# Reordering the opening of a fused forward-and-backward kernel: which load, which product and which table come first

## The chip, the cores and the metric

The kernel runs on one core of one Trainium2 chip. The metric is the device time of one execution in microseconds (us), lower is better. The core has a matrix engine (TensorE; PE in the profile, its weight loads PEld), a vector engine (VectorE, DVE), a scalar engine (ScalarE, ACT), a general engine (GpSimd, POOL) and a queue engine that issues most transfers (SyncE, SP). Each engine works through its own instructions in a fixed order and waits on semaphores for the others. PSUM is the memory that TensorE writes to; a result there is "evicted" by VectorE or ScalarE. Chip memory is reached by DMA only.

## What is computed

The reference is a block with a spectral mixer and an MLP, both modulated by a condition vector `c`, together with all its gradients (one sequence of 2048 rows, width 512, MLP width 1792, bfloat16):

```python
mod = (silu(c) @ w_mod).reshape(1, 6, 1, -1)
sa, ca, ga, sb, cb, gb = (mod[:, i] for i in range(6))
h = layernorm(x) * (1 + ca) + sa
x = x + ga * irfft2(rfft2(h) * (w_r + 1j * w_i))
h = layernorm(x) * (1 + cb) + sb
x = x + gb * (relu(h @ w1 + b1) ** 2 @ w2 + b2)
# outputs: x and, for grad_out, the gradients of A_x, w_r, w_i, w1, b1, w2, b2, c, w_mod
```

## The kernel before

**Stages.** The 2048 rows are 16 tiles of 128 rows, handled in pairs, and four blocks `b` of four tiles. The Fourier transforms are products with sine tables that the kernel makes itself: GpSimd writes integer patterns (`iota`), VectorE turns them into phases (a multiply-add and a bitwise and), ScalarE takes `Sin`. The tables are `TA`/`TAT` (`build_ta`), `Cd` (`build_cd`), the middle table `LF` (`build_lf`, four quarters `q`, patterns from `iotas_lf`) and `Cf` (`build_cf`).

**The opening** is this. `c` and `b1` are loaded into one small tile `vrow` (L560, L561), turned to columns by one TensorE transpose into `vrow_ps` (L589), and ScalarE makes the sigmoid (L590) and `scb`, silu(c) repeated over 128 columns (L593). `mod_row(j)` (L604) is one of the six modulation rows: four products of 512 columns with a 512-column part of `w_mod` (tile `wm`), spread over all partitions and evicted into `modb`. Row 1 is `ca`, row 5 is `gb`. `gb` is then needed as a column over partitions, so four one-column products turn row 5 round (L621) and VectorE doubles it into `gb2x` (L623).

**The row stage** works on pairs of row tiles: statistics (`row_stats`, L638 and L639 on VectorE, then four small GpSimd operations), normalisation (`row_norm`, L650 on VectorE or L652 on ScalarE), times 1+ca (L656), a fold (`fold1`, L250 and L251), and the first transform (`spec_f1_half`, L286 and L287, into `psA`), evicted by ScalarE into `UT` (L288, `utcs`).

**The fill.** The gradient of the MLP's inner layer, `grad_out` times `w2` transposed, needs nothing of the forward path. Both operands come by transposing DMAs: `w2T` (L580, two halves) and `gT[b]` (L577, one per block, in two buffers, so that block 2 waits for the products of block 0 and block 3 for those of block 1). VectorE scales `gT[b]` by `gb2x` (`scale_g`, L629). `back_products(b)` then makes 14 results `fc` of four products each (L714), 56 a block and 224 in all, evicted into `gab`: every third by VectorE (L717), the others by ScalarE (L719). They have a very late priority, so the scheduler puts them into gaps of TensorE that it expects.

**What follows.** Modulation rows 0, 4, 3, 2 and a row `dcrow` made of them (L692, L693); `spec_f23`, the two further transforms for eight groups `gi` (L324, evicted to `AE` by L329; L310, evicted to `Xs` by L312), each followed by a complex product with the spectral weights (`cmul`, L420 to L423); `spec_g1` (L345, L358), `spec_g2` (L376, `Tsb` L379) and `spec_g3` (L387) back; the second layernorm; then the MLP forward (L886), back, and the weight gradients, to the end. The first L886 product stands behind all 224 fill products.

**What sets the order.** A scheduler orders the instructions of each engine when the program is built, from its own estimates and from priorities: `tc.high_priority()` pulls a part forward, `Priority(tc, LATE)` pushes it back, and `with tc.issue_after(K[...])` keeps an instruction behind a named one. Transfers on SP and ScalarE are issued in the order of that engine's instructions, so a wait of one holds back those behind it. Tiles of a pool share `bufs` buffers: a new tile waits until the last reader of the one that it replaces is done.

## Time and profile before

| | |
|---|---|
| time, three runs | 419.98, 422.49, 424.95 us (median 422.49) |
| span of the profiled execution (first to last instruction) | 416.3 us; a time of its own is not listed beside the span |
| TensorE clock granted | 1.000 |
| busy share: PE, PEld, DVE, ACT, POOL | 94, 47, 83, 67, 15% |
| data moved by DMA | 101.11 MB, 243 GB/s on average |
| share of the largest DMA queue (q1) | 84.1% of 16 engines |
| `gT` (block 0) transposing DMA, time on SP's queue | 6.85 us from 2.22 |
| first product of the row stage; first fill product | 14.60; 16.27 us |

A line of the profile's groups or of its instructions in order of time has: the start, the time of one or several instructions, engine, source line, operation, tile written, tiles read, shape, count, and in brackets how long the engine had stood idle before and what ended that. An "xN" joins N instructions; their times overlap by the pipeline of the engine, so the distance of two starts is often shorter than the time of one.

### The profile page before, as it was taken

To read this page: it belongs to the slowest core of one execution; us is meant where nothing else is said; L and a number is where in the kernel's file an instruction comes from. 1 tells how busy PE (TensorE), PEld (TensorE's weight loads), DVE (VectorE), ACT (ScalarE), POOL (GpSimd) and SP (SyncE) were. 2 spreads that over 40 slices of the span, in tenths; PEclk is the share of its full clock that TensorE was granted. 3 is DMA by queue.
4 is the path that set the end of the run, shared out by engine and by line. 5 is a ranking of instruction groups with operands and counts; after the bars stand their busy time and mean duration, and the time that the engine had idled before them with its cause. 6 is when DMAs were issued, how large, how long until landed. Compare 5 with 4: busy or idle time off the path is not lost. (4 is left out here: it accounts for less than half of the span.)

```text
span 416.3 us, 7175 instructions
## 1 busy us (share of the span) xinstructions
PE 391.7 (94%) x2387; PEld 197.6 (47%) x2407; DVE 343.7 (83%) x827; ACT 277.1 (67%) x495; POOL 60.6 (15%) x147
## 2 busy tenths in 40 slices
PE   2789999999899999999999999999999999999996
PEld 0345445664444444444444444445555665444444
DVE  6899868977988578988897998964999784877885
ACT  4568699868884079338924776545655567897785
POOL 7437950000000000000000000001314520000000
PEclk9999999999999999999999999999999999999999
DMA  8999899979199459949976997998999999999994
GB/s 240 232 261 298 237 213 313 323 239 240 40 331 324 126 161 276 248 128 204 288 227 194 201 291 278 291 213 245 287 280 283 350 265 227 223 269 223 239 266 143
DMA packets 143923, 101.11 MB, mean 243 GB/s; under 512 B 99049, under 2 KB 126830, under 8 KB 143630
## 3 DMA queue, kind: packets, MB, share of 16 engines
q1 hardware_dynamic: 140394, 92.96, 84.1%
q0 software_dynamic: 2784, 7.10, 5.6%
q10 hardware_dynamic: 708, 0.59, 0.5%
q8 instruction: 19, 0.31, 0.3%
q14 instruction: 18, 0.15, 0.1%
HBM read 35.44 MB, written 41.60 MB: 185 GB/s over the span
## 5 line engine op out<-in xcount | busy, mean ns | idle before, releaser
L714 PE MATMUL mm<-gT,w2T 128*128 128x512 bf16 x224 | 57.9, 382 | 4.5 <-ACT gab L719 4.2
L1144 PE MATMUL mm<-gab,h_sb 128*128 128x448 bf16 x256 | 50.9, 352 | 0.0
L1232 PE MATMUL mm<-g_sb,hn 128*128 128x512 bf16 (+1 forms) x250 | 49.6, 352 | 0.8 <-ACT gw L1234 0.4
L915 PE MATMUL og<-w1T,gab 128*128 128x512 bf16 x219 | 49.9, 379 | 0.3
L915 PE MATMUL og<-w,h 128*128 128x512 bf16 x216 | 49.1, 379 | 0.4
L886 PE MATMUL mm<-h2T,w 128*128 128x512 bf16 x164 | 40.2, 379 | 0.5 <-ACT r L888 0.3
L1232 PEld LDWEIGHTS <-hn 128*128 128x128 bf16 x256 | 24.4, 98 | 23.4 <-issue 2.0
L1144 PEld LDWEIGHTS <-h_sb 128*128 128x128 bf16 x256 | 24.6, 98 | 21.8 <-issue 0.8
L886 PEld LDWEIGHTS <-w 128*128 128x128 bf16 x224 | 21.3, 98 | 27.7 <-issue 4.9
L915 PEld LDWEIGHTS <-h 128*128 128x128 bf16 x224 | 21.7, 98 | 25.6 <-DVE h L890 0.6
L915 PEld LDWEIGHTS <-gab 128*128 128x128 bf16 x224 | 21.6, 98 | 25.5 <-DVE gab L894 1.0
L714 PEld LDWEIGHTS <-w2T 128*128 128x128 bf16 x224 | 21.2, 98 | 24.2 <-issue 7.9
L888 ACT ACTIVATE r<-mm,b1col 128x512 bf16<-128x512 f32 x41 | 27.4, 688 | 6.3 <-DVE gab L894 3.3
L294 POOL MEMSET AE<- 128x2 bf16 x4 | 0.3, 103 | 188.5 <-DMA gh_dram<-gab 188.5
L928 ACT CAST G<-og 128x512 bf16<-128x512 f32 x16 | 9.2, 580 | 22.2 <-PE og L915 22.2
L329 ACT ACTIVATE AE<-psB 128x1024 bf16<-128x1024 f32 x16 | 21.8, 1363 | 1.8 <-PE psB L324 0.9
L719 ACT CAST gab<-mm 128x512 bf16<-128x512 f32 x36 | 21.0, 593 | 2.6 <-PE mm L714 2.3
L890 DVE TENSOR_TENSOR h<-r 128x1024 bf16<-128x1024 bf16 x28 | 19.2, 686 | 2.6 <-ACT r L888 2.5
L1148 ACT CAST gw<-mm 128x448 bf16<-128x448 f32 x16 | 8.6, 537 | 18.4 <-PE mm L1144 18.4
L477 DVE SCALAR_TENSOR_TENSOR gm_junk<-wmc,onef,gmbc 128x512 bf16<-128x512 bf16 x24 | 18.0, 750 | 3.3 <-ACT gmbc L467 2.2
L894 DVE TENSOR_TENSOR gab<-r,gab 128x1024 bf16<-128x1024 bf16 x28 | 19.2, 684 | 0.0
L379 ACT ACTIVATE Tsb<-psT 128x512 bf16<-128x512 f32 x32 | 18.5, 603 | 0.6 <-ACT utcs L368 0.5
(292 smaller groups left out, 818.5 us busy)
## 6 DMA issues: line engine op xcount, KB each, us to landing
h_dram<-h SPq DMA_DIRECT2D x28, 256.0 KB, 3.2
gh_dram<-gab SPq DMA_DIRECT2D x28, 256.0 KB, 3.6
w<-in_B_w_dram SPq DMA_DIRECT2D x2, 1792.0 KB, 9.0
wmc<-in_w_mod_dram SPq DMA_DIRECT2D x12, 256.0 KB, 5.8
wz_dram<-Z SPq DMA_DIRECT2D x8, 258.0 KB, 3.8
xs_dram<-Xs SPq DMA_DIRECT2D x8, 258.0 KB, 4.0
Z<-wz_dram SPq DMA_DIRECT2D x8, 258.0 KB, 6.0
Xb<-xs_dram SPq DMA_DIRECT2D x8, 258.0 KB, 8.2
```

The source lines that it names most:

```text
L329: nc.scalar.activation(dst, ps.rearrange("p r (s e f) -> p (r s) e f", s=2, e=2), AF.Copy, scale=EF_S)
L379: K["Tsb"] = nc.scalar.activation(Tsb, ps, AF.Copy, scale=EF_S).ins
L477: nc.vector.scalar_tensor_tensor(out=junk, in0=wmc[:, i, :], scalar=K["onef"], in1=gmbc, op0=ALU.mult, op1=ALU.mult, accum_out=self.gsc[:, ...
L714: nc.tensor.matmul(ps, lhsT=w2T[:, dc, fc * P:(fc + 1) * P], rhs=gT[b][:, :, dc, :], start=(dc == 0), stop=(dc == 3))
L719: nc.scalar.copy(out=gaT[b][:, fc, :], in_=ps)
L886: nc.tensor.matmul(ps, lhsT=w1[:, dc, (fc + i) * P:(fc + i + 1) * P], rhs=h2T[b][:, :, dc, :], start=(dc == 0), stop=(dc == 3))
L888: nc.scalar.activation(r[:, i, :], ps, AF.Relu, bias=b1col[:, fc + i:fc + i + 1])
L890: nc.vector.tensor_tensor(h2, r, r, op=ALU.mult)
L894: K["gh"] = nc.vector.tensor_tensor(gh, r, gh, op=ALU.mult).ins
L915: nc.tensor.matmul(ps, lhsT=lhs(fc), rhs=rhs[:, fc, :], start=(fc == 0), stop=(fc == NFC - 1))
L1144: nc.tensor.matmul(ps[:, 0:W4], lhsT=h2_sb[:, t, dc * P:(dc + 1) * P], rhs=ghn[t // 4][:, t % 4, fs], start=(t == 0), stop=(t == NT - 1))
L1232: nc.tensor.matmul(ps[:, 0:w], lhsT=hns[fc][:, t, :], rhs=g_sb[:, t, c:c + w], start=(t == 0), stop=(t == NT - 1))
```

## The change

- Loads: `c` goes first on SP's queue, alone; `b1` goes into a tile of its own (`brow`) on ScalarE's queue. Then the first four row tiles, the weights of row 5, `gT[0]`, the weights of row 1, and `w2T` in three pieces (3, 4 and 7 of its 14 parts) with the later row tiles between and behind them.
- The gate column: instead of row 5, its eviction and four one-column products, sixteen one-column products of the weights with the column `sc` = silu(c). Row 5 is made later, after the row stage. The transpose of `b1` goes there too.
- `scale_g(0)` no longer stands behind the statistics; `scale_g(2)` stands behind a product of the row stage in place of the phases of `LF`.
- `build_lf` is split: `build_lf_phase` (phases and `Sin`, now straight into `LF`) is written ahead of the row stage; the multiplication by signs and masks stays where it was, in place. The patterns for it are made first on GpSimd.
- Four small PSUM tiles share one name, `sm_ps`, with two buffers. `TA` is held behind the sigmoid.

```diff
@@ build_ta
+    with tc.issue_after(K["sig"]):
+        nc.scalar.activation(TA[:, 0], v, AF.Sin, scale=TWO_PI / 128, bias=K["npi"])
...
+def build_lf_phase(tc, K, cpool, g, krs):
...
+    for q in range(4):
+        v = g.tile([P, 2, 4, P], I16, name="lf_v", bufs=2)
+        for i in range(2):
+            V.tensor_scalar(v[:, i], krs[q].rearrange("p a h x u -> p (a h) (x u)"), t, ph[:, i:i + 1], op0=ALU.mult, op1=ALU.add)
+        if q == 0:
+            V.tensor_scalar(v[:, :, 0, 2:64:4], v[:, :, 0, 2:64:4], 512.0, None, op0=ALU.add)
+        K["lf_v"] = V.tensor_single_scalar(v, v, 2047, op=ALU.bitwise_and).ins
+        K["lf_w"] = nc.scalar.activation(LF[:, 4 * q:4 * q + 4, 0:2, :], v.rearrange("p i n x -> p n i x"), AF.Sin,
+                                         scale=TWO_PI / 2048, bias=K["npi"]).ins
...
@@ the opening
-    nc.scalar.dma_start(vrow[0:4, :], c.rearrange("b (dc p) -> (b dc) p", p=P))
-    nc.scalar.dma_start(vrow[4:4 + NFC, :], B_b1.rearrange("(fc p) -> fc p", p=P))
+    nc.sync.dma_start(vrow, c.rearrange("b (dc p) -> (b dc) p", p=P))
...
-    nc.sync.dma_start(x_sb[:, 0:4, :], x_view[:, 0:4, :])
-    nc.sync.dma_start(wmt[0][:, :, D:2 * D], wm_view[:, :, D:2 * D])
-    nc.scalar.dma_start(wmt[2][:, :, D:2 * D], wm_view[:, :, 5 * D:6 * D])
-    nc.sync.dma_start(x_sb[:, 4:8, :], x_view[:, 4:8, :])
...
+    load_x(0, 4)
+    load_mod(5)
+    load_gT(0)
+    load_mod(1)
+    load_w2T(0, 3)
+    load_w2T(3, 7)
+    load_x(4, 4)
+    load_w2T(7, NFC)
+    load_x(8, 4)
+    load_x(12, 4)
+    nc.scalar.dma_start(brow, B_b1.rearrange("(fc p) -> fc p", p=P))
+    load_mod(4)
+    load_gT(1)
+    load_mod(0)
+    load_wm(1)
+    load_gT(2)
+    load_gT(3)
...
+        K["sig"] = nc.scalar.activation(sigcol, pv, AF.Sigmoid).ins
+        nc.vector.tensor_copy(ccolf, pv)
+        sc = p0.tile([P, 4], BF16, name="sc")
+        nc.vector.tensor_tensor(sc, sigcol, ccolf, op=ALU.mult)
...
+    build_ta(tc, K, constp, gen, psM)
+    build_cd(tc, K, lfp, gen)
+    lf_io, lf_kr = iotas_lf(tc, gen)
+    cf_dr = iota_cf(tc, gen)
+    lf_ph = build_lf_phase(tc, K, lfp, gen, lf_kr)
...
-        mod_row(1)
-        mod_row(5)
-        psc = psM.tile([P, 4], FP32, name="modc_ps", bufs=1)
+        psc = psM.tile([P, 4], FP32, name="sm_ps")
         for cc in range(4):
-            nc.tensor.matmul(psc[:, cc:cc + 1], lhsT=modb[0:1, GB_B, cc * P:(cc + 1) * P], rhs=K["ones_col"][0:1, :], start=True, stop=True)
+            for dc in range(4):
+                nc.tensor.matmul(psc[:, cc:cc + 1], lhsT=wmt[2][:, dc, D + cc * P:D + (cc + 1) * P], rhs=sc[:, dc:dc + 1], start=(dc == 0), stop=(dc == 3))
         gb2x = constp.tile([P, 4], FP32, name="gb2x")
         nc.vector.tensor_scalar(gb2x, psc, 2.0, None, op0=ALU.mult)
+        mod_row(1)
...
-            with tc.issue_after(K[("stats", "stats", "lf_v", "cmul")[b]]):
+            with tc.issue_after(K[("stats", "stats", "f1v", "cmul")[b]]) if b else ExitStack():
...
     row_stats(0)
+    scale_g(0)
...
-        for j in (0, 4, 3, 2):
+        for j in (0, 4, 3, 2, 5):
             mod_row(j)
+        pb = psM.tile([P, NFC], BF16, name="sm_ps")
+        nc.tensor.transpose(pb, brow, K["ident"][0:NFC, 0:NFC])
+    nc.vector.tensor_copy(b1col, pb)
...
-    build_lf(tc, K, lfp, gen, *lf_io)
+    build_lf(tc, K, gen, lf_io, *lf_ph)
```

In the program as it is built after the change, the orders that matter are these. TensorE: transposes, the sixteen products, row 1, 34 fill products, then the first transform; 66 fills stand ahead of the last transform (66 before the change too), 89 ahead of the dc row's use (84 before), 116 at the end of `spec_f23` (144 before), 126 at the end of `spec_g1` (150 before). VectorE: three phases ahead of `TA`'s copies, the rest between the first statistics and the first fill evictions, three fill evictions ahead of the first fold; the scaling of `gT[3]` inside the last `cmul`. ScalarE: row 1's eviction, three `Sin`, two fill evictions, the fourth `Sin`. SP: the DMA of `gT[3]` behind the sixth `xs_dram` store, where it waits for the last product of block 1, fill 112.

## The prediction, made before the changed kernel was run

> **What bounds the kernel now.** I read the page first, then busy time by stage, the instructions in order of time on each engine, and what TensorE waited for.

> ```profile
> PE 391.7 (94%) x2387; PEld 197.6 (47%) x2407; DVE 343.7 (83%) x827; ACT 277.1 (67%) x495; POOL 60.6 (15%) x147
> ```

> TensorE is busy for 94% of the span, so a microsecond is won or lost only where TensorE stands idle. I cut the span at its own milestones: first row transform (14.60), last one (41.20), dc row (50.70), inverse transform (79.87), its row step (89.70), first forward MLP product (113.77).

> ```profile
> core 0: us, PE busy (x) PEld busy (x) DVE busy (x) ACT busy (x) POOL busy (x), PEclk, DMA share, GB/s
> 0.00:14.60 14.60, 4.44 (x15) 1.36 (x15) 9.75 (x54) 6.75 (x12) 9.87 (x54) 1.00 0.99 245
> 14.60:41.20 26.60, 23.74 (x130) 13.20 (x131) 24.56 (x68) 19.32 (x34) 14.38 (x32) 1.00 1.02 264
> 41.20:50.70 9.50, 9.45 (x65) 4.25 (x63) 8.06 (x41) 6.78 (x12) 9.03 (x16) 1.00 0.83 239
> 50.70:79.87 29.17, 27.04 (x193) 15.85 (x192) 22.93 (x64) 27.70 (x42) 6.68 (x12) 1.00 1.04 267
> 79.87:89.70 9.83, 9.82 (x103) 7.19 (x104) 9.26 (x18) 5.51 (x10) 0.00 (x0) 1.00 1.01 346
> 89.70:113.77 24.07, 22.47 (x139) 10.95 (x140) 19.23 (x48) 20.69 (x41) 0.00 (x0) 1.00 0.57 140
> ```

> The second stage is VectorE's (24.56 of 26.60), the fourth ScalarE's (27.70 of 29.17). The 224 products of L714 (the "fill": gradient times w2T) are spread between these stages by the scheduler, and all of them stand ahead of the first forward product, before and after. Busy TensorE is flattered by pipelining, so I count work by spacing: twelve fill products take 2.75 us, (2.75-0.38)/11 = 0.215 us each; a 256-column product 0.11, a 128-column one 0.055. By that, the second stage holds 66 fills and 64 transforms, 14.2+7.0 = 21.2 us in 26.6: 5.4 us are idle. The stage from 50.70 holds 23.8 in 29.2; the last 21.0 in 24.1.

> The opening is a chain of waits:

> ```profile
> 5.81 0.17 PE L589 MATMUL vrow_ps<-ident,vrow 18*128 18x18 bf16 x1 [5.81 <-DMA vrow<-in_B_b_dram]
> 10.88 1.87 PE L604 MATMUL mod_ps<-wm,scb 128*128 128x512 bf16 x4 [0.78 <-ACT modb L606]
> 13.75 0.26 PE L621 MATMUL modc_ps<-ones_col,modb 1*128 1x1 bf16 x4 [1.00 <-ACT modb L610]
> 14.60 0.39 PE L286 MATMUL psA<-TA,fold_u 128*128 128x256 bf16 x1 [0.59 <-DVE fold_u L250]
> 23.79 2.75 PE L714 MATMUL mm<-gT,w2T 128*128 128x512 bf16 x12 [0.36 <-ACT gab L719]
> ```

> **The change, step by step.** *Opening.* c goes first, without b1, so the transpose need not wait for the second small load; from c's issue at 0.75 the sigmoid can start up to some 1.3 us sooner, but this ends no wait that I price, since the gate column then waits for its weights. SP's queue gains three issues (c, the gate weights, one more w2T piece) of about 0.41 us (row L567), which delay the first x by 0.45. The gate column replaces mod_row(5), its eviction and four products by sixteen one-column products. Bytes ahead of the gate weights shrink to c and one x tile: 1.05 MB. 142 GB/s in the first five us and 333 in the next five put that at 6.0; the first x tile, 3.7 by the same count, was waited for until 5.41 (1.7 more), so I take 7.4. Sixteen one-column products have no row; below, four L621 took 0.26 us (0.065 each, so 1.0); above, mod_row's weight loads follow at 0.25 to 0.32 (so 4 to 5). I take 0.1, nearest to the 98 ns of a weight load: 1.6. The gate scale is then ready at about 9.0 instead of 14.05.

> [...]

> *VectorE.* The four table phases are moved from 40 to 57 us, where VectorE has gaps (19.23 of 25 busy from 40 to 65), into and before the row stage, where it has none:

> ```profile
> 40.54 0.41 DVE L222 TENSOR_SCALAR lf_v<-lf_kr,lf_tf,lf_ph 128x512 int16<-128x512 int16 x1
> 42.30 0.43 DVE L225 TENSOR_SCALAR lf_v<-lf_v 128x1024 int16<-128x1024 int16 x1
> ```

> By the start of what follows each, eight L222 at 0.34, four L225 at 0.34 and a short one are 4.2 us. In the built order all of them stand ahead of the first fold. VectorE's idle before the last fold (end 40.4) is now 4.2 us: 0.58 for TA, 1.08 for the gate, 0.55 and 0.58 for evictions and others. After, I find in order: 2.1 waiting for the gate scale (its queue runs dry near 6.7), 0.9 for the eviction of the first fill, which stands ahead of the statistics, 0.9 for that of the fourth, 1.0 for the rest: 4.9, bounds 3 and 7. The 0.56 it waits for the first x at 4.84 is now filled with phases, 0.6 back. So the row stage ends later by 4.2+(4.9-4.2)-0.6 = 4.3 us, bounds 4.2+(3-4.2)-0.6 = 2.4 and 4.2+(7-4.2)-0.6 = 6.4. Who waits: the first transform stands behind 34 fills on TensorE and behind three fill evictions on VectorE; I place it at 22 to 24 instead of 14.60. The fills ahead of it cannot repay this: 66 stand before the last transform in both orders. x tiles 4, 8 and 12 move behind pieces of w2T; the second, issued at 13.20 before, comes out near 19, needed at 26, so it has cover; without it, VectorE stands up to 2 us.

> *ScalarE.* Four Sin (L227, 1.15 us) leave the ScalarE stage; in the opening they sit behind the eviction of mod_row(1), and the second fill's eviction waits behind three of them: in the 0.9 above. The stage shrinks to 8 x (1.20+0.95) for AE and Xs, 5 x 0.48 for fill evictions, 2.4 for start and end: 22.0 instead of 29.2. That is no gain by itself: the built order puts 27 fills in it, not 60; the 33 taken out (7.1 us) go behind it: 10 in place of 6 in the inverse transform, 98 in place of 74 after.

> *mod_row(5)* now stands behind f1, where TensorE has no gap (9.45 of 9.50): 4 x 0.215 = 0.86.

> *gT(3).* This is what is late next. The fourth transposed gradient reuses the second's buffer, so its DMA waits for fill 112. Before, that fill ran near 58 and the DMA was issued at 68.11:

> ```profile
> 68.11 2.82 SPq L577 DMA_TRANSPOSE gT<-in_grad_out_dram  x1
> ```

> After, fill 112 stands between the spectral products of groups 6 and 7, and VectorE's scaling of gT(3) stands inside the last complex product, ahead of the inverse transform's evictions. The DMA landed 5.4 us after its issue; VectorE reaches it about 3.0 after fill 112 (ScalarE's eviction of a fill and two Xs, 1.45, then one 0.61 product, and 0.9 of pipeline). VectorE stands 2.4 us, and TensorE with it, whose inverse transform has four buffers. Bounds: 0 (fill 112 early) and 5.

> [...]

> *Given back.* With more fills in the last stage TensorE's 3.1 us idle there shrink: 1.0 (0 to 2.5). The new order also does 1.3 us of later work before the fills end and frees VectorE for the MLP: 0.5.

> **Sum:** 4.3+0.86+2.4-1.0-0.5 = +6.1 us on a span of 416.3, so 422.4. What lies around the span of this execution is not shown; the runs' median, 422.49, is 6.2 above the span (their lowest 3.7). I add the difference to the median: 428.6. Bounds of the terms: 2.4+0.86+0-2.5-0.5 = +0.3 and 6.4+0.86+5 = +12.3, where nothing is given back.

> **Rivals.**
> *Faster, 417.4.* One mechanism: the row stage ends sooner. If the gate scale is there at 8, the phases fit wholly into VectorE's idle opening and fills begin by 12 without holding the folds, then the last fold comes at 37.4 (-3.0), fill 112 runs early (0), and the last stage gives back 2.5: -3.0+0.86-2.5-0.5 = -5.1. For it: VectorE is idle a third of the first 14.6 us (9.75 busy), ScalarE half. Against: 4.2 us of phases, and fill evictions ahead of the folds. It decides from a first transform before 16 us.
> *Next to nothing, 423.9.* The opening swallows most of the phases (+1.0), gT(3) costs 1.0: 1.0+0.86+1.0-1.0-0.5 = +1.4. For it: all the work is conserved. Against: the row stage's VectorE share.
> *The gate comes no earlier, 431.2.* If the gate weights land at 10.0 as now (second group of L604 waited then), the scale comes at 11.6, and VectorE, with the scale ahead of its statistics, stands 2.6 us more: 6.1+2.6 = +8.7. For it: DMA share 0.99 in the opening. Against: fewer bytes ahead.

> **How the numbers follow.** Forecast (428.6) 0.42, late gate 0.15, nothing 0.29, faster 0.14. This measurement tells about 1% (4.2 us) from no change. Slower by more than that holds the first two, 0.57; within it 0.29; faster 0.14. The range, 419.0 to 434.0, reaches over the second rival and the late gate, leaves out most of the faster case and the top of the bounds. The forecast and the late gate alone reach from 425 to 434.

> **What would show it.** Right: gate scale near 9; first transform after 20 and the last between 43 and 47; the AE stage of about 22 us; VectorE waiting for gT's DMA once, for 1 to 5 us, near 78; 98 fills after 89. Wrong: a last transform before 41, no wait for gT(3), or TensorE idle after 89.7 down by more than 3 us.

## The result, and the profile after

The changed kernel takes 435.09 us (median; 434.06 to 436.86) against 421.44 us for the kernel before beside it on the same chip: a ratio of 1.0306, interval [1.0236, 1.0376]. It is slower by some 13 us (13.7 by the medians) where 6.1 were forecast; the range ended at 434. The sign and the places of the losses were right; the size of the largest one was not, nor what one DMA waits for. Medians are over all runs of a kernel; a ratio leaves out the few runs that the record marks as slow.

The span of the profiled execution is 433.6 us. From here on every run lists its time beside its span, and the time is some 1.8 us longer. The profile shown of before, span 416.3, therefore stands for 418.1 us, less than any time listed for that kernel. Two more profiles of the unchanged kernel have spans of 422.8 and 422.7; I compare with the first of these, the second profile. Its own time, 424.56, is 3.1 us above the median of the kernel before given here, so that the spans differ by less (10.8) than the medians (13.7).

The page of the kernel after, engines and granted clock:

```profile
PE 396.1 (91%) x2400; PEld 198.7 (46%) x2420; DVE 346.4 (80%) x828; ACT 277.6 (64%) x495; POOL 59.6 (14%) x147
...
PEclk9997999969999999999999999999999999999999
```

TensorE works no less, but its share falls from 94 to 91%, and in two slices its clock is not full. Busy time by stage, after, then the second profile of before, cut at the same milestones (first transform, last one, dc row, inverse transform, its row step, end of the fills):

```profile
core 0: us, PE busy (x) PEld busy (x) DVE busy (x) ACT busy (x) POOL busy (x), PEclk, DMA share, GB/s
0.00:25.00 25.00, 11.39 (x57) 4.81 (x58) 20.38 (x80) 13.14 (x20) 10.40 (x56) 1.00 0.97 214
25.00:48.47 23.47, 16.94 (x98) 9.52 (x97) 20.13 (x58) 17.29 (x30) 14.09 (x33) 0.85 0.90 256
48.47:60.06 11.59, 11.54 (x74) 5.18 (x72) 9.98 (x55) 9.14 (x18) 10.62 (x20) 1.00 0.86 275
60.06:81.70 21.64, 19.26 (x160) 12.76 (x159) 14.07 (x28) 19.92 (x29) 3.91 (x7) 1.00 1.07 273
81.70:99.42 17.72, 13.55 (x107) 8.64 (x107) 10.27 (x21) 5.52 (x10) 0.00 (x0) 0.81 0.76 230
99.42:129.86 30.44, 29.61 (x176) 14.12 (x176) 25.10 (x61) 25.91 (x51) 0.00 (x0) 1.00 0.41 96
```

```profile
core 0: us, PE busy (x) PEld busy (x) DVE busy (x) ACT busy (x) POOL busy (x), PEclk, DMA share, GB/s
0.00:16.21 16.21, 4.44 (x14) 1.35 (x15) 12.47 (x54) 6.75 (x12) 9.53 (x54) 1.00 1.00 240
16.21:43.61 27.40, 24.79 (x131) 13.70 (x132) 24.69 (x69) 19.69 (x34) 15.06 (x32) 1.00 0.94 247
43.61:52.94 9.33, 9.33 (x64) 4.14 (x62) 7.83 (x39) 6.62 (x12) 8.52 (x15) 1.00 0.84 248
52.94:82.14 29.20, 27.05 (x192) 15.86 (x192) 22.92 (x65) 27.72 (x42) 7.11 (x13) 1.00 1.01 279
82.14:91.95 9.81, 9.79 (x102) 7.17 (x103) 9.27 (x18) 5.49 (x10) 0.00 (x0) 1.00 0.99 339
91.95:115.58 23.63, 22.12 (x135) 10.76 (x136) 18.95 (x46) 20.37 (x40) 0.00 (x0) 1.00 0.56 126
```

Read by the starts of the milestones (last transform 48.36 after, 43.35 before; last fill's end 129.94 and 115.58):

| stage | before, 2nd profile | after | difference | forecast |
|---|---|---|---|---|
| start to last row transform | 43.35 | 48.36 | +5.0 | +4.3 |
| to the dc row | 9.59 | 11.70 | +2.1 | +1.9 (row 5, five more fills) |
| to the inverse transform | 29.20 | 21.64 | -7.6 | -7.2 |
| to its row step | 9.81 | 17.72 | +7.9 | +3.3 (0.86 for fills, 2.4 for `gT[3]`) |
| to the last fill | 23.63 | 30.52 | +6.9 | +5.5 (24 fills, 1.3 of early work, -1.0) |
| the rest | 307.22 | 303.66 | -3.6 | -1.8 |
| sum | 422.8 | 433.6 | +10.8 | +6.0 |

Not all of this is the change: the rest took 302.8, 307.2 and 307.8 us in three profiles of one kernel, the one before. The one stage that is far off is the inverse transform. There, the fills 109 to 112, SP's queue, VectorE and TensorE, and then the clock in short stretches:

```profile
78.24 1.02 PE L736 MATMUL mm<-gT,w2T 128*128 128x512 bf16 x4
...
81.82 0.40 SPq L766 DMA_DIRECT2D xs_dram<-Xs  x1
82.27 4.05 SPq L579 DMA_TRANSPOSE gT<-in_grad_out_dram  x1
```

```profile
88.37 1.14 DVE L649 TENSOR_SCALAR gT<-gT,gb2x 128x512 bf16<-128x512 bf16 x4 [4.57 <-DMA gT<-in_grad_out_dram]
```

```profile
90.77 1.01 PE L351 MATMUL psG<-LG,Z 128*128 128x256 bf16 x4 [4.16 <-DVE utcs L356]
...
93.27 5.27 PE L351 MATMUL psG<-LG,Z 128*128 128x256 bf16 x32
```

```profile
88.00:92.00 4.00, 1.23 (x10) 0.50 (x9) 3.63 (x10) 0.18 (x1) 0.00 (x0) 0.72 0.99 279
92.00:96.00 4.00, 4.00 (x18) 2.40 (x17) 1.87 (x3) 1.57 (x3) 0.00 (x0) 0.50 0.69 278
```

VectorE reaches the scaling of the fourth gradient block at 83.80, 1.5 us after its DMA was issued, and stands until it lands, 6.1 after the issue. The inverse transform's evictions (`utcs`) are queued behind it, so TensorE stands 4.16 us, and after that runs at half clock: 32 products take 5.27 us that take 3.66 in the kernel before. The part on the change has this DMA wait for fill 112; but that fill ended at 79.26, and the DMA went out 3.0 us later, directly behind the sixth store of `Xs` on SP's queue.

### The profile page after: what moved, and what is told of

Same layout as the page of the kernel before. It is cut to its first block, busy times and chain, and to the rows that moved or that the text cites. A ratio compares the mean times of both kernels' runs of the same rounds, so it can differ in the third digit from the quotient of the medians.

```text
span 433.6 us, 7207 instructions
## 1 busy us (share of the span) xinstructions
PE 396.1 (91%) x2400; PEld 198.7 (46%) x2420; DVE 346.4 (80%) x828; ACT 277.6 (64%) x495; POOL 59.6 (14%) x147
## 5 line engine op out<-in xcount | busy, mean ns | idle before, releaser
L736 PE MATMUL mm<-gT,w2T 128*128 128x512 bf16 x224 | 59.2, 388 | 3.9 <-ACT gab L741 1.8
L358 ACT CAST utcs<-psG 128x512 bf16<-128x512 f32 x18 | 10.2, 587 | 15.6 <-PE psG L351 15.6
```

The costliest lines, as they stand in the source:

```text
L358: nc.scalar.copy(out=dst, in_=src)
L736: nc.tensor.matmul(ps, lhsT=w2T[:, dc, fc * P:(fc + 1) * P], rhs=gT[b][:, :, dc, :], start=(dc == 0), stop=(dc == 3))
```

## Experiments on the inverse transform

**A third gradient buffer.** `gT` gets three buffers, so that the fourth block needs no product to end; to make room, one integer tile of `build_cd` shares a name with another and one of `build_ta` is worked in place.

```diff
-        gT.append(w2gp.tile([P, TB, 4, P], BF16, name="gT", bufs=2))
+        gT.append(w2gp.tile([P, TB, 4, P], BF16, name="gT", bufs=3))
```

> The changed kernel with three buffers for the transposed gradient instead of two (two scratch tiles of the table builders share space to make room), so that the DMA of block 3 waits for the products of block 0 and not for fill 112. The built order is the same up to the inverse transform. Theory A (VectorE's wait for that DMA and the slow TensorE clock behind it cost a third of the loss): no VectorE wait for the gradient's DMA, the inverse transform's stage 17.7 -> about 10.8 us, granted clock there 1.00 instead of 0.81, time 435.1 -> about 428.5. Theory B (the loss is that 33 fill products were pushed behind the spectral stage, and TensorE works them off anyhow): the wait goes, but no more than 1.5 us of time, 433.5 or above.

Measured: 442.83 us, ratio 1.0451 [1.0391, 1.0511]. The stage did fall, from 17.7 to 10.7 us without the wait for the DMA; but the time rose. With the block there early the scheduler put 92 fills in a row ahead of the first `psY`, and behind them TensorE waited for ScalarE (total, times, longest):

```profile
PE psY L393 <- ACT Tsb L385: 7.8, 8, 1.4
```

So the stage agreed and the total was decided by an order that the edit had not meant to touch. It says nothing on what the wait is worth.

**The scaling later.** The same wait taken away with the order untouched up to the inverse transform; the fills on the fourth block move with its scaling:

```diff
-            with tc.issue_after(K[("stats", "stats", "f1v", "cmul")[b]]) if b else ExitStack():
+            with tc.issue_after(K[("stats", "stats", "f1v", "cast")[b]]) if b else ExitStack():
...
-            if gi == 4:
-                back_products(NB - 1)
...
     spec_g1(tc, K, Z, CS)
+    back_products(NB - 1)
```

> The kernel after, with VectorE's scaling of the fourth gradient block, and the fill products on it, put behind the inverse transform's evictions; the order up to the inverse transform is untouched. Theory A (VectorE's 4.6 us wait for the late block starves the inverse transform, and TensorE's half clock in that stage follows from the 4.2 us gap): the stage from the first psG to the first psT shrinks from 17.7 us to 10 or 11, its granted clock from 0.81 to 0.95 or more, the wait for the block's DMA is gone or below 1 us, the span falls by 5 to 7 us, time about 429. Theory B (the stage is long for another reason, the evictions or the moved transfers): the stage stays over 14 us and the time within 2 us of 435.

Measured: 429.15 us, ratio 1.0149 [1.0096, 1.0201]. The stage by its busy times, and its 32 products:

```profile
82.44:92.01 9.57, 9.56 (x102) 7.03 (x103) 9.17 (x18) 4.91 (x9) 0.00 (x0) 1.00 1.04 305
```

```profile
87.47 3.66 PE L351 MATMUL psG<-LG,Z 128*128 128x256 bf16 x32
```

17.7 us became 9.57, the clock is 1.00 and the products are back at 3.66. Theory A is shown: the place of this one scaling, with the fills that hang on it, costs 6 of the 13 us, counted from the medians (435.1 to 429.2). The edit takes the gap and the slow clock away together; what each is worth alone was not measured.

## Experiments on the opening

What follows is read with VectorE's and TensorE's instructions in the opening of the kernel after:

```profile
9.37 0.15 DVE L642 TENSOR_SCALAR gb2x<-sm_ps 128x4 f32<-128x4 f32 x1
...
15.30 0.73 DVE L213 TENSOR_SCALAR lf_v<-lf_kr,lf_tf,lf_ph 128x512 int16<-128x512 int16 x2 [2.73 <-ACT LF L217]
```

```profile
7.93 0.57 PE L640 MATMUL sm_ps<-sc,wm 128*128 128x1 bf16 x16 [0.84 <-DVE sc L609]
...
25.00 0.27 PE L292 MATMUL psA<-TA,fold_u 128*128 128x256 bf16 x1
```

The gate scale is there at 9.37. But VectorE then stands 2.73 us: there are two phase buffers, and ScalarE's `Sin`, which frees them, is queued behind row 1's eviction at 13.46.

**No phase buffer.** The phases are written into the table itself, and `Sin` works in place.

```diff
-        v = g.tile([P, 2, 4, P], I16, name="lf_v", bufs=2)
+        v = LF.bitcast(I16)[:, 4 * q:4 * q + 4, 0:2, :].rearrange("p n i x -> p i n x")
```

> The changed kernel with the phases written into the table LF itself, where Sin then works in place, so that VectorE need not wait for one of two phase buffers that Sin still reads behind the eviction of modulation row 1. The scheduler then puts the first row transform behind 16 fills instead of 34. Theory A: VectorE's 2.7 us wait at 12.6 goes, the row stage ends near 45.5 instead of 48.5, time about 432 (-2 to -3.5). Theory B: VectorE reaches the same first fill evictions no sooner, the row stage ends after 47.5, time within 1 us of 435.1.

Measured: 431.99 us, ratio 1.0203 [1.0143, 1.0264]. The first transform comes at 21.11 instead of 25.00, the dc row at 57.41 instead of 60.06, and the time falls by 3.1 us; all four times lie below the four of the kernel after. This wait is real and I had not seen it. Part of the 3.1 can be the order, since 16 fills now stand ahead of the first transform in place of 34; the two were not separated.

**Patterns.** Beside it I suspected GpSimd: L102 and L130, two steps of integer work on VectorE, stand from 3.37 to 7.15 in the kernel after, while GpSimd writes its patterns. Here are the first profile of before, and the second:

```profile
3.39 0.22 DVE L102 TENSOR_SCALAR ta_v<-ta_v 128x128 int32<-128x128 int32 x1
3.52 0.79 DVE L129 TENSOR_SCALAR gen_v<-cd_fr,cd_d 128x256 int32<-128x256 int32 x2
```

```profile
3.39 3.71 DVE L102 TENSOR_SCALAR ta_v<-ta_v 128x128 int32<-128x128 int32 x1
3.52 3.71 DVE L129 TENSOR_SCALAR gen_v<-cd_fr,cd_d 128x256 int32<-128x256 int32 x1
```

The kernel after with the order of patterns of before, in `iotas_lf`:

```diff
+    sm = g.tile([P, 6, 4], I32, name="lf_sm")
+    nc.gpsimd.iota(sm[:, 0, :], pattern=[[1, 4]], base=0, channel_multiplier=0)
...
     krs = []
     for q in range(4):
...
-    sm = g.tile([P, 6, 4], I32, name="lf_sm")
...
```

> The changed kernel with the small patterns of GpSimd ahead of the large ones again, as before the change; no other engine's order changes. Theory A (VectorE stood from 3.4 to 7.1 us because GpSimd ran its large patterns without a gap at that time): the two instructions on ta_v and gen_v take together about 1.3 us instead of 6.6, the sigmoid's product sc comes before 6 us, gate scale near 8.2, row stage ends 1 to 2.8 us sooner, time 432.3 to 434. Theory B (they waited for something else, such as a transfer): they take as long as in the changed kernel, time 435.1 within 0.7.

Measured: 435.13 us, ratio 1.0291 [1.0239, 1.0343]; L102 3.71 and L130 3.96 us. The order of the patterns is not it. Then the patterns held back altogether, by copies from VectorE's result into the pattern tiles ahead of each pattern:

```diff
+        nc.vector.tensor_copy(kr[:, :, :, :, 0:64:32].rearrange("p a h x u -> p (a h x u)"), K["cdv"][:, 0:16])
...
+    nc.vector.tensor_copy(sm.rearrange("p a b -> p (a b)"), K["cdv"][:, 0:24])
```

> The kernel after, with GpSimd's patterns for the middle tables made to wait for the end of VectorE's integer table work (five small copies give the dependence). Theory A (that work, L102 and L130, stands some 5.5 us because it overlaps GpSimd's pattern stream): the two take below 1.2 us together, VectorE is free 2.5 us sooner, the last transform comes 2 to 3 us sooner than at 48.5 and the time is about 432. Theory B (something else holds them, a load for one): they still take over 3 us each.

Measured: 436.43 us, ratio 1.0296 [1.0231, 1.036]. The stretch is gone (L102 0.39, L130 0.65), so the overlap makes it; and nothing is won, since VectorE now waits 4.16 us instead of 2.73 for the phase buffer. The two had covered each other. To learn whether the stretch belongs to the change at all, the kernel before was profiled twice more, and run with its own patterns held back in the same way:

> The kernel before, unchanged, profiled once more. Theory A (the 3 us that VectorE's two integer instructions stand beside GpSimd's patterns belong to the program's usual execution, and the profile shown of before was one without them): L102 and L129 take over 2.5 us, the first transform comes near 17 instead of 14.6, span 418 to 421. Theory B (the stretch comes with the change): L102 0.2, L129 below 1, span 416 to 417.

> The kernel before, unchanged, a third profile, for how often the two integer instructions stand long: the same two theories with the same numbers as for the second profile.

> The kernel before, with GpSimd's patterns for the middle tables behind VectorE's integer table work (five small copies give the dependence); TensorE's order is that of the kernel before. Theory A (the stretch is usual in the kernel before, too, and ends when VectorE can start the statistics): L102 and L129 below 1.2 us together, statistics at 5.5, time 2 to 3 us below the kernel before, ratio 0.993 to 0.996. Theory B (row 1's weights end the opening anyway, near 10.9): ratio within 0.003 of 1.

Measured: L102 3.71 and 3.70, L129 3.96 in both; spans 422.8 and 422.7; first transform at 16.21 in both. It is the usual execution of the kernel before, and the one profile that I forecast from was the exception. Held back, the time is 423.87 us, ratio 1.0015 [0.9978, 1.0052], first transform at 15.94. That is Theory B's number but not its reason: VectorE's first fold stands behind the gate scale, and this waits for row 5's eviction (`modb`, L613), not for row 1.

```profile
15.09 0.26 PE L624 MATMUL modc_ps<-ones_col,modb 1*128 1x1 bf16 x4 [2.56 <-ACT modb L613]
...
15.39 0.16 DVE L626 TENSOR_SCALAR gb2x<-modc_ps 128x4 f32<-128x4 f32 x1 [1.38 <-PE modc_ps L624]
15.47 0.41 DVE L253 TENSOR_TENSOR fold_u<-h 128x512 bf16<-128x512 bf16 x1
```

So the stretch explains neither the loss nor, alone, the short span of the first profile.

## Which part costs what

**Phases back.** In the kernel after, `build_lf_phase` is called just ahead of `build_lf` again, behind the row stage.

```diff
-    lf_ph = build_lf_phase(tc, K, lfp, gen, lf_kr)
...
+    lf_ph = build_lf_phase(tc, K, lfp, gen, lf_kr)
     build_lf(tc, K, gen, lf_io, *lf_ph)
```

> The changed kernel with the table phases and their Sin back behind the row stage, all else kept: loads in the new order, gate column by one-column products, row 5 late. Theory A (the phases in the row stage are the main cost, and with them gone fill 112 runs early enough for the last gradient DMA): row stage ends between 41 and 43, no wait for the gradient's DMA above 1 us, time 420 to 424. Theory C (the loads and the gate column, which put fills and their evictions ahead of the first folds, are the main cost): row stage ends after 45, time 428 or above.

Measured: 425.86 us, ratio 1.0078 [1.0042, 1.0114]: nine of the 13 us go with the phases, the rest does not. Neither theory holds as it stands, since the last transform still comes only at 46.72 and VectorE still waits 2.05 us for the fourth gradient block. And the nine are not a second cost beside the 6 above: the block's DMA now goes out at 74.07, and the inverse transform takes 11.3 us instead of 17.7, so that most of the nine is that same stage.

**Phases and first gradient block back.** As above, and `scale_g(0)` at the third pair again.

```diff
     row_stats(0)
-    scale_g(0)
...
+        if t == 4:
+            scale_g(0)
```

> The kernel after, with the table phases back behind the row stage, and with the scaling of the first gradient block back where it stood before the change (behind the third pair's statistics, so that no fills stand ahead of the first transform); c alone, the order of the loads, the one-column gate products and row 5 behind the row stage are kept. Theory A (VectorE's added work in the row stage is all that costs there): first transform at 15 or 16 us, last one below 42.5, dc row 10.5, time 422 to 425, ratio 1.00 to 1.006. Theory B (the new order of the loads costs the rest, 3 us, too): last transform at 44 or later and time 426 as with the phases alone moved.

Measured: 429.91 us, ratio 1.0125 [1.0056, 1.0194]: no better, which Theory A had excluded. The first transform came at 19.44 and not at 15 or 16, and VectorE's wait ahead of it names the cause:

```profile
18.36 0.69 DVE L657 BATCH_NORM_STATS2 l_st<-x_sb 128x6 f32<-128x512 bf16 x1 [3.52 <-DMA x_sb<-in_A_x_dram]
```

The second tile of x, issued at 1.67 before the change, is now issued at 12.69, behind `gT[0]`, row 1's weights and two pieces of `w2T`. But this is not where the profile falls behind that of the run before, whose first transform came later still (21.25) and whose inverse transform began no sooner (83.46; here 83.03). It is the inverse transform, 15.0 us against 11.3. VectorE stands 4.11 us for the fourth block instead of 2.05, and 32 products take 5.09 us at a granted clock of 0.51:

```profile
83.07 1.14 DVE L648 TENSOR_SCALAR gT<-gT,gb2x 128x512 bf16<-128x512 bf16 x4 [4.11 <-DMA gT<-in_grad_out_dram]
```

```profile
89.03 0.22 PE L364 MATMUL psF<-LG,Z 128*1 128x128 bf16 x2 [1.44 <-DMA LG<-LF_dram]
...
92.04 5.09 PE L351 MATMUL psG<-LG,Z 128*128 128x256 bf16 x32
```

```profile
92.00:95.00 3.00, 3.00 (x15) 2.12 (x14) 1.72 (x4) 0.69 (x2) 0.00 (x0) 0.51 0.96 314
```

The times of the two runs are not clearly apart: their intervals overlap.

**Row 1's weights first**, ahead of x, in that kernel, and row 1 ahead of the gate column:

```diff
+    load_mod(1)
     load_x(0, 4)
     load_mod(5)
     load_gT(0)
-    load_mod(1)
...
+        mod_row(1)
         psc = psM.tile([P, 4], FP32, name="sm_ps")
...
-        mod_row(1)
```

> As the run with phases and gate blocks late, and the weights of modulation row 1 are loaded first behind c, ahead of the first x tile, and row 1 is computed ahead of the gate column. Theory A (row 1's eviction ends the chain to the first transform): row 1 is there by 9 us, the first transform comes 1.5 us sooner, at 13 to 14, and the time is 1 us below that run. Theory B (VectorE's statistics end it, and these wait for the first x tile, now 1 us later): first transform not sooner, time the same or 1 us above.

Measured: 427.59 us, ratio 1.0119 [1.0074, 1.0164]; row 1's eviction 2.6 us sooner (10.80), first transform at 19.19. Row 1 did not set it; the second x tile did (4.09 us of wait). The inverse transform took 11.2 us again.

**One part alone on the kernel before.** First the loads, with every engine's order of instructions as it was:

```diff
     nc.sync.dma_start(x_sb[:, 0:4, :], x_view[:, 0:4, :])
-    nc.sync.dma_start(wmt[0][:, :, D:2 * D], wm_view[:, :, D:2 * D])
-    nc.scalar.dma_start(wmt[2][:, :, D:2 * D], wm_view[:, :, 5 * D:6 * D])
-    nc.sync.dma_start(x_sb[:, 4:8, :], x_view[:, 4:8, :])
...
+    load_mod(5)
+    load_gT(0)
+    load_mod(1)
+    load_w2T(0, 3)
+    load_w2T(3, 7)
+    load_x(4, 4)
...
```

> The kernel before, with the order of the loads taken from the kernel after (gate weights and first gradient block ahead of row 1's weights, the second x tile behind two of the three pieces of w2T); every engine's order of instructions is that of the kernel before. Theory A (the second x tile, issued at 1.7 before and near 13 now, holds VectorE's third statistics until 18): VectorE waits 3 to 4 us for the tile, the first transform comes near 19.4 and the last near 46, time 4 to 5 us above the kernel before, ratio 1.010 to 1.012. Theory B (the order of the loads is harmless, what held the runs with late phases was the gate column and the table work ahead): first transform by 16, ratio within 0.004 of 1.

Measured: 426.70 us, ratio 1.012 [1.0091, 1.015]; the row stage begins 3.8 us later (20.02) and is no longer than it was (26.7 for 27.4), as Theory A said:

```profile
17.62 0.69 DVE L651 BATCH_NORM_STATS2 l_st<-x_sb 128x6 f32<-128x512 bf16 x1 [4.91 <-DMA x_sb<-in_A_x_dram]
```

Then the gate column, and the phases; with the phases come, as in the kernel after, the order of the patterns and the place of `scale_g(2)`:

```diff
         mod_row(1)
-        mod_row(5)
...
-            nc.tensor.matmul(psc[:, cc:cc + 1], lhsT=modb[0:1, GB_B, cc * P:(cc + 1) * P], rhs=K["ones_col"][0:1, :], start=True, stop=True)
+            for dc in range(4):
+                nc.tensor.matmul(psc[:, cc:cc + 1], lhsT=wmt[2][:, dc, D + cc * P:D + (cc + 1) * P], rhs=scb[:, dc, 0:1], start=(dc == 0), stop=(dc == 3))
...
-        for j in (0, 4, 3, 2):
+        for j in (0, 4, 3, 2, 5):
```

> The kernel before, with the gate column alone taken from the kernel after: sixteen one-column products on the weights, row 5 with its eviction moved behind the row transforms; loads, phases and the place of the gradient's scaling as before. Theory A (the part is worth what it moves): the scale is ready 1 to 2 us sooner, which nothing on the path uses, since fills stand behind the first transforms; row 5's four products cost 0.86 behind the row stage; time 0 to 1.5 us above the kernel before, ratio 1.000 to 1.004. Theory B (row 5's eviction held the first transform): first transform 0.6 us sooner and the time at or below the kernel before.

```diff
     nc.vector.tensor_copy(scf, scb[:, :, 0])
+    lf_ph = build_lf_phase(tc, K, lfp, gen, lf_kr)
...
-    build_lf(tc, K, lfp, gen, *lf_io)
+    build_lf(tc, K, gen, lf_io, *lf_ph)
```

> The kernel before, with the table phases and their Sin alone moved ahead of the row stage, as in the kernel after; loads, gate column and gradient scaling as before. Theory A (the phases are VectorE work in a stage that VectorE sets): last transform 4 to 7 us later than at 41.1, and what the ScalarE stage wins goes behind it; time 5 to 8 us above the kernel before, ratio 1.012 to 1.019. Theory B (with the x tiles and the gate at their old times VectorE's idle opening takes the phases): last transform within 2 us of 41.1, ratio within 0.004 of 1.

Measured: 426.58 us, ratio 1.0135 [1.0103, 1.0167], for the gate column; 430.66 us, ratio 1.0229 [1.0194, 1.0264], for the phases. The gate column costs 5 us, more than either theory allowed: the scheduler placed 58 fills ahead of the last transform in place of 66 and 140 ahead of the inverse transform's row step in place of 150, and the row stage was not shorter for it (28.1 us). The phases alone cost as much as their return gave back above, nine, but not in the same place: here the inverse transform takes 9.4 us, and 107 fills are done at its row step in place of 150, 43 at 0.215 us, 9.2 us.

Alone, the three parts cost 5.1, 5.0 and 9.1 us, 19 in sum; the whole change, with its smaller parts, 13. None of the three alone has the long inverse transform (9.8, 10.4 and 9.4 us against 17.7): that cost comes only with the parts together. In the opening they cover one another: in the kernel after, VectorE is busy with phases and fill evictions while the x tile travels. Moving only that tile's load in the kernel after shows it:

```diff
+    load_x(4, 4)
     load_gT(0)
     load_mod(1)
     load_w2T(0, 3)
     load_w2T(3, 7)
-    load_x(4, 4)
```

> The kernel after, with one load moved: the second tile of x is issued ahead of the first gradient block, as before the change, instead of behind two pieces of w2T; every engine's order is untouched. Theory A (in the kernel after, the late tile lies behind the phases, fills and evictions that hold VectorE until 18 us anyway): first transform within 1 us of 25.0, time within 2 us of the kernel after, 433 to 437. Theory B (the tile sets the start of the row stage): first transform 2 us sooner or more and time 432 or below.

Measured: 435.58 us, ratio 1.0323 [1.027, 1.0376]. Nothing is won (first transform at 26.32), as Theory A said.

## Versions with the waits removed

Three combinations of the edits above. The first is the kernel with phases and first gradient block back, the x tile's load moved and the scaling later.

> The run with phases and gate blocks late, and the second tile of x ahead of the first gradient block, and the fourth gradient's scaling behind the inverse transform. Theory A (in that run VectorE's 3.5 us wait for the tile held the first transform at 19.4): the wait is gone, the first transform comes at 15 to 16, the last one at 42 to 43, the stage from the first psG to the first psT takes 9.5 to 10.5, and the time is 420 to 423, at or below the kernel before. Theory B (the gate weights and the loads behind them set the stage): last transform still at 45 or later and time 425 or more.

Measured: 428.77 us, ratio 1.0142 [1.0102, 1.0181]. The waits for the x tile and for the fourth block are gone, but VectorE now waits 2.95 us for row 1's eviction; the first transform comes at 17.35, the last only at 45.1. These are the numbers of Theory B.

The second is the kernel after with the phases written into the table, the x tile's load moved and the scaling later.

> The kernel after with its early gate, early fills and early phases kept, and three waits removed: phases written into the table itself (no phase buffer), the second x tile ahead of the first gradient block, the fourth gradient's scaling behind the inverse transform. If the waits add up as measured one by one (3.0 for the phase buffer, 1.3 for the tile, 6 for the gradient), the time is about 425; the phases' own VectorE work, some 4 us in the row stage, then remains of the loss. Rival: the early fills and their evictions hold the folds as well, and the time stays above 428.

Measured: 427.40 us, ratio 1.012 [1.0069, 1.0171]; 425 was the sum of the three waits, 428 the rival's; it lies between them.

The third is the first one with the patterns held back, and row 1's weights ahead of the tile:

```diff
     load_x(0, 4)
     load_mod(5)
+    load_mod(1)
+    load_x(4, 4)
     load_gT(0)
-    load_mod(1)
```

> The run with the second x tile early and the gradient late, and besides it the weights of modulation row 1 ahead of the second x tile, and GpSimd's patterns behind VectorE's integer table work. Theory A (with the tile there, statistics start when VectorE is free of the table work, and that is 2.5 us sooner without the overlap): first transform at 12.5 to 13.5, time 1 to 2 us below the run without these two, 418 to 421. Theory B (row 1's weights end the chain at 10.8 whatever VectorE does): first transform at 14 to 15 and the time the same within 1 us.

Measured: 427.40 us, ratio 1.0119 [1.0071, 1.0166]. The first transform comes at 13.35, sooner than in any other profile, and the last at 43.6, later than in the kernel before: an early start of a stage that VectorE sets and that now waits for a later x tile (1.83) and for fills (2.5) ends no sooner.

What is left in these versions can be followed with one number: the start of the inverse transform's row step less 0.215 us for each fill done by then, that is, TensorE time gone to anything but fills.

| kernel | row step | fills | less fills | above before | time above before |
|---|---|---|---|---|---|
| before, 2nd profile | 91.95 | 150 | 59.7 | | |
| after | 99.42 | 126 | 72.3 | 12.6 | 13.7 |
| gradient late | 92.01 | 121 | 66.0 | 6.3 | 6.3 |
| phases late | 94.74 | 138 | 65.1 | 5.4 | 3.4 |
| three waits removed | 89.44 | 121 | 63.4 | 3.7 | 4.6 |
| x early, gradient late | 92.34 | 127 | 65.0 | 5.3 | 6.0 |
| best order | 91.13 | 127 | 63.8 | 4.1 | 4.6 |
| before, gate column | 94.31 | 140 | 64.2 | 4.5 | 5.0 |
| before, load order | 95.08 | 150 | 62.8 | 3.1 | 5.1 |
| before, phases early | 89.36 | 107 | 66.4 | 6.7 | 9.1 |

The version with three waits removed reaches its row step 2.5 us before the kernel before does, and loses: 29 more fills are still to do, 6.2 us. Fills that find no gap early stand on the path later. To within 2.5 us the last two columns agree; the rest was not followed. (The other two profiles of before would give 57.4 and 59.0 in place of 59.7.) The run with three gradient buffers does not fit: 5.8 us by this number, 20.3 by its time, since its 92 fills in a row stand behind the row step. No version is faster than the kernel before. Why the scheduler's placement with the gate column alone costs 5 us was not taken apart further; row 5's four products, 0.86 us, are in it.

## Why the prediction was right or wrong, point by point

- **Gate scale near 9:** right, 9.37, but in part by luck. Its term was mis-sized without harm: the sixteen products took 0.57 us, not 1.6, and were done at 8.50. VectorE came to the scale only behind phases.
- **Row stage, +4.3:** +5.0 against the usual profile of before. The size is nearly right and the working is not; that they meet is luck. I had found 4.9 us of idle VectorE after the change in four waits. The first, 2.1 for the gate scale, did not occur: the two integer steps held VectorE until 7.15, and its queue never ran dry there. The phase buffer was not among them (2.73 us, worth 3.1 of time by the run without it, changed order included). I had written that the `Sin` sit behind row 1's eviction, and did not ask who waits for the `Sin`.
- **The x tiles:** the step names tiles 4, 8 and 12 as moved and prices only the one issued at 13.20, tile 8. Tile 4 moved from 1.67 to 12.69; the new load order alone, whose wait is that of this tile, is worth 5.1 us. It did no harm to the number only because VectorE was held by the other two until then, as the run with this load alone moved shows; that was luck too.
- **First transform, last transform:** predicted after 20 and between 43 and 47; measured 25.00 and 48.36. The upper end was missed by 1.4.
- **dc row and row 5:** right, +2.1 for +1.9.
- **The ScalarE stage of about 22 us:** right, 21.64, and right that it is no gain by itself: 24 fewer fills stand ahead of the row step.
- **`gT[3]`, +2.4 (0 to 5):** the term that failed. The place was right, and that VectorE's wait there holds TensorE; VectorE waited once, 4.57 us, inside the 1 to 5 named. Three things were wrong. The sum counts from fill 112, as if the DMA went out when that fill ended; it ended at 79.26, and SP's queue let the DMA out at 82.27. (In the kernel before that fill ended at 61.81, not near 58, and the DMA at 68.11 stood directly behind another transfer too.) The landing then took 6.1 us and not 5.4, so that from fill 112 the data came after 9.1 us and VectorE after 4.5, where 5.4 and 3.0 were summed. And I set TensorE's loss equal to VectorE's wait. TensorE lost a gap of 4.16 us and then ran at half clock; the stage grew by 7.9 where 3.3 had been summed, and the run with the scaling later won back 6.
- **Given back, 1.5 and the early work:** TensorE's idle time in the last fill stage shrank from 1.5 to 0.8 us by stage less busy. By the sum's own count it did not: the stage grew by 6.9, and the 24 fills and the 1.3 of early work make 6.5 without anything given back. The rest of the span moved by more between profiles of one kernel than the 0.5 that I took.
- **Base of the sum:** the profiled span, 416.3, was 6 below those of two later profiles, and adding the difference to the median was the right way round it. I noted 6.2 us between median and span as unexplained; it meant that this execution was not a usual one. The range stopped at 434.0, below the sum's own upper bound (422.5 + 12.3 = 434.8); the measured 435.1 lies above both.
- **The rivals:** the faster case needed a first transform before 16; next to nothing needed the opening to swallow the phases; neither came near. The late gate did not happen.

## What to carry to other kernels

Ask of each instruction that may wait for a transfer what stands behind it on its engine, and of the transfer what stands ahead of it in its queue; here one scaling of 1.1 us, placed ahead of evictions instead of behind them, cost 6 us, by the profile some 4 of them as a gap and some 2 through products that then ran slowly. When a stage is set by one engine, work moved into it is paid, and when several delays overlap, removing one can show nothing: put each part alone on the old kernel too. And when the profiled span and the measured times do not fit, profile the same kernel again before building a sum on it.

## What the runs showed of the hardware

```profile
40.00:46.00 6.00, 4.71 (x21) 2.79 (x22) 5.12 (x16) 4.25 (x7) 4.60 (x11) 0.55 0.44 139
```

```profile
126.00:135.00 9.00, 5.77 (x37) 3.74 (x37) 8.48 (x23) 7.30 (x15) 0.00 (x0) 0.50 1.17 235
```

- **Weight loads.** Fifteen loads of 128 columns in the kernel after took 0.48 us with 0.10 for one, so (0.48-0.10)/14 = 0.027 us from one to the next. I had taken the 0.1 of a single load for each of the sixteen products.

```profile
7.93 0.48 PEld L640 LDWEIGHTS <-wm 128*128 128x128 bf16 x15 [0.58 <-issue]
```

- **VectorE beside GpSimd's patterns.** In all profiles but one in which they overlap, the two integer steps of VectorE stand 2.7 to 4.0 us and are done between 6.47 and 7.48, about when GpSimd's patterns end (6.70 in the kernel after, 6.72 with the phases alone back); without the overlap they take 0.39 and 0.65. In the exception, the first profile of before, they took 0.22 and 0.79, and it was GpSimd patterns that were longer (one 0.58 in place of 0.34 us). So three profiles of one program show the long VectorE steps twice and not the third time. That the overlap makes the VectorE steps long is shown by the runs with the patterns held back; by what means was not shown.
